# Seven-product stage of h kept in program order, with two attention visits a period and the second pair's x sums on VectorE in place

## The chip, the cores and the metric

The kernel runs on one core of a Trainium2 chip. TensorE (PE) multiplies, VectorE (DVE) and ScalarE (ACT) read its PSUM banks, GpSimd (POOL) works from SBUF alone, and SyncE (SP) issues the transfers. Each engine takes its instructions strictly in order, so an instruction that waits holds up all that stand behind it on that engine. The metric is the time of one execution on the device in microseconds; lower is better.

## The reference, cut to what matters

```python
state = gamma * state + einsum('bhd,bhe->bhde', k[t], v[t])   # retention, 4 batches, 8 heads, 768 tokens
y[t]  = scale * einsum('bhd,bhde->bhe', q[t], state)
x = y.transpose(0, 2, 1, 3).reshape(3072, 512)
h = x @ w_in                  # 512 -> 2048
g = h - tanh(h)
x = g @ w_out                 # 2048 -> 512
h = x @ w_in2                 # 512 -> 1024; then softmax-weighted h, layer norm, @ w_out2 -> 512
```

All is fp32. A product of two fp32 tiles is taken as three matmuls: each tile is split into a high part (a cast to fp32r on ACT) and the low rest (a subtraction on DVE), and the products high by high, high by low and low by high are added in PSUM.

## The kernel before

Attention works in 24 units: six chunks c of 128 tokens by four batches b. A unit is visited twice by PE. The first visit, "sc", forms the scores and the new state, which DVE turns into `pr`, `sb` and `sa` (L327 to L338). The second, "out", forms the outputs; ACT copies them from the two banks into x (`xf`, L299), and DVE adds the second part from the same banks (L307). Both visits use the same two PSUM banks (pool `ps_a`), so the next sc visit can start only when the copies and the additions of the visit before are done.

The tokens lie in six blocks of 512 (`SB`). The product h = x @ w_in is done for two blocks at a time (a pair) against two tiles of w_in, with seven products P1 to P7 for each two-by-two block of tiles instead of eight (L758, six matmuls of 128x128 by 128x512 each). The seven need sums and differences of the tiles of w_in (`wsum`, L544 to L547, class `Factors`) and of x (`x_sums`, L605, L610 on DVE and L601 on POOL), and each of these is split into high and low (`wch`/`wcl`, `xh`/`xl`, by `parts`, L165 and L166; `put_x` does it for x).

The stage of h that the change touches has 16 periods n. Periods 0 to 7 work on the first pair (blocks 2 and 3) against eight groups j of w_in, and 8 to 15 on the second pair (blocks 4 and 5) against the same groups, stored to DRAM (`wcd`, `store_w`) and loaded again (`load_wl`). A period issues P2(n), P5(n), P4(n-1), P6(n), P3(n-1), P1(n+1) and P7(n), in banks of a pool of six (`ps_h`). P1, P5 and P6 are read from their bank by ACT into `part` (`keep`, L768), because the bank goes on being added to. `summed` (DVE, L784) adds bank and part to `hs`; `finish` takes the tanh (ACT, L774) and the difference (L776, on POOL after P2, P3 and P7, on DVE after P4), and the result `g` goes to DRAM (`gd`). The buffers for `part`, `hs`, `th` are a ring of 15 (`t2`), those for weights and x a ring of 40 (`t4`); SP keeps at most eight transfers under way.

In the same periods the last 16 attention visits (units 16 to 23, whose x are blocks 4 and 5) stand between the products, three a period in periods 0 to 5, and `Factors(n+1)` prepares the weights of the next period. In the last period, the first `gp` (splits of g loaded back) and `w` (splits of w_out) for the following stage, x = g @ w_out (`py`, L382), are made.

The order on PE and SP is that of the program. What ACT, DVE and POOL do in this stage is put in order by the framework's scheduler when the program is built; an instruction that goes through `pin(..., True)` keeps its place in program order among the others that do, and `fix` does so where `late[0]` is set. Before, `late[0]` is set only near the end of the kernel.

Of the kernel before, what the change touches and what calls it, by code (L numbers as in the profile page):

```python
# [36 lines left out]
P = 128  # L37
# [52 lines left out]
def body(ctx: ExitStack, tc, z, w_in, w_out, w_in2, w_out2, g_ln, cst, tab, out):  # L90
# [144 lines left out]
    def prepare(k, own, wide=False, fixed=True):  # L235
# [12 lines left out]
        ), wide and fixed)  # L248
        src = zv[k][:, 1, :, :].rearrange("q p (h d) -> q (p h) d", h=2)
        c0 = C_VS + c * H  # L250
        for h in range(own):
            pin(nc.scalar.activation(
                v[:, h, :], src[:, h, :], AF.Copy, scale=con[:, c0 + h : c0 + h + 1]
            ), wide and fixed)
        if own < H:
            pin(nc.gpsimd.tensor_tensor(
                v[:, own:, :], src[:, own:, :],
                con[:, c0 + own : c0 + H].unsqueeze(2).to_broadcast([P, H - own, D]), ALU.mult,
            ), wide and fixed)
        vs[k] = v  # L260

    def unit(ko, ks, hold=False, pool=ps_r, tag="r", opool=ps_r, engs=None, amid=None):
# [4 lines left out]
        if ko is not None:  # L267
# [29 lines left out]
            if c:  # L297
                for h in range(2):
                    pin(nc.scalar.copy(xf[:, h, :, :], fr[h]), amid)  # L299
            else:  # L300
                for h in range(2):
                    pin(nc.scalar.copy(xf[:, h, :, rows(1)], fr[h][:, :, rows(1)]), amid)
                pin(nc.scalar.copy(xa[:, :, rows(0)], ya[0]), amid)
            if amid:
                amid()
            for ab in steps:
                pin(nc.vector.tensor_tensor(  # L307
                    xa[:, :, rows(ab)], xa[:, :, rows(ab)], ya[ab], ALU.add
                ), amid)
            if not hold:  # L310
                split_x(c, b, xf, engs or (nc.gpsimd, nc.gpsimd), amid)
        if ks is not None:
# [13 lines left out]
            for h in range(2):  # L326
                pin(nc.vector.tensor_tensor(  # L327
                    pr[:, h, :, :], sc[h], mask.unsqueeze(1).to_broadcast([P, NP, D]), ALU.mult
                ), amid)
            pt[ks] = pr  # L330
            sb[ks] = stp.tile([P, NP, D], F32, tag="sb", name="sb", bufs=3)
            if c == 0:
                nc.scalar.copy(sb[ks], gn[0])
            else:
                nc.vector.tensor_tensor(sb[ks], sa[ks], gn[0], ALU.add)
            if c < NC - 1:
                sa[ks + B] = stp.tile([P, NP, D], F32, tag="sa", name="sa")
                nc.vector.tensor_tensor(sa[ks + B], sb[ks], gn[1], ALU.add)  # L338
# [193 lines left out]
    class Factors:  # L532
# [6 lines left out]
        def sums(self):  # L539
# [4 lines left out]
            nc.vector.tensor_tensor(t[:, 0, :], a21, a22, ALU.add)  # L544
            nc.vector.tensor_tensor(t[:, 1, :], t[:, 0, :], a11, ALU.subtract)
            nc.vector.tensor_tensor(t[:, 2, :], a11, a21, ALU.subtract)
            nc.vector.tensor_tensor(t[:, 3, :], a12, t[:, 1, :], ALU.subtract)  # L547

        def split(self, i):
            g, half = divmod(i, 2)  # L550
            if half == 0:
                self.parts[g][:] = [t4([P, 4, 256], F32R, "wc" + n) for n in "hl"]
# [6 lines left out]
            h, o = (u[:, 2 * half : 2 * half + n, :].rearrange(flat) for u in self.parts[g])  # L559
            parts(h, o, src, nc.vector)  # L560
# [6 lines left out]
    def combine_w(j):  # L567
        w = Factors(j)
        w.sums()
        for i in range(4):  # L570
            w.split(i)
# [21 lines left out]
    def x_sums(p, step):  # L593
# [3 lines left out]
        def apart(out, a, b):  # L597
            for i in range(2):
                for k in range(0, SB, SB // 2):
                    at = slice(k, k + SB // 2)  # L600
                    nc.gpsimd.tensor_tensor(out[:, i, at], a[:, i, at], b[:, i, at], ALU.subtract)  # L601

        if step == 0:
            t1 = t4([P, 2, SB], F32, "xt")
            nc.vector.tensor_tensor(t1, b12, b11, ALU.subtract)  # L605
            apart(b12, b22, b12)
            sums[p] = {P1: b11, P2: b21, P3: b22, P5: t1, P7: b12}
        else:
            t2_, t4_ = (t4([P, 2, SB], F32, "xt") for _ in range(2))
            nc.vector.tensor_tensor(t2_, b22, sums[p][P5], ALU.subtract)  # L610
# [125 lines left out]
    visits = []  # L736
    for k in range(4 * B, NU):
        visits += [("sc", k), ("out", k)]
    per = [[] for _ in range(NJ1)]
    for i, v in enumerate(visits):  # L740
        per[i // 3].append(v)

    def visit(v):
        kind, k = v
# [21 lines left out]
    def keep(ph):  # L766
        t = t2([P, SB], F32, "part")
        nc.scalar.copy(t, ph)  # L768
        return t

    def finish(s, f, h, eng):

        th = t2([P, SB], F32, "th")
        nc.scalar.activation(th, h, AF.Tanh)  # L774
        g = th if eng is nc.vector else h
        eng.tensor_tensor(g, h, th, ALU.subtract)  # L776
# [5 lines left out]
    def summed(ph, part):  # L782
        h = t2([P, SB], F32, "hs")
        nc.vector.tensor_tensor(h, ph, part, ALU.add)  # L784
# [35 lines left out]
    def split_wo(f):  # L820
        wo[f] = stage3(wof[f], None, nc.vector, False)

    def begin(n):
# [3 lines left out]

    x_at = {
        (NJ1 - 1, P2): P1, (NJ1 - 1, P5): P2, (NJ1 - 1, P6): P5,
        (NJ1, P2): P6, (NJ1, P5): P7, (NJ1, P6): P4, (NJ1, P7): P3,  # L830
    }

    def after(n, m):
        if (n, m) in ((NJ1 - 2, P5), (NJ1 - 1, P2)):
            x_sums(2, n - (NJ1 - 2))
        if (n, m) in x_at:
            put_x(2, x_at[n, m], nc.vector)

    begin(0)
    for n in range(len(q) + 1):  # L840
        now, was = n < len(q), n > 0
        p, j = q[n] if now else (NSB, 0)
        todo = list(per[j]) if p == 1 else []
# [3 lines left out]

        def piece(i):
            if new:
                new.split(i) if i >= 0 else new.sums()  # L850
# [9 lines left out]
        if n == len(q) - 1:  # L860
            for i in range(2):
                split_p(i)
                split_wo(i)
        if now:
            b3 = bank()
            product(wl[n], p, P2, b3)
            finish(2 * p, j, summed(b3, p1.pop(n)), nc.gpsimd)
            piece(-1)
            after(n, P2)
            b2[n] = bank()  # L870
# [3 lines left out]
            piece(0)  # L874
            after(n, P5)
            if todo:
                visit(todo.pop(0))
        if n == len(q):
# [3 lines left out]
            split_p(2)  # L882
            split_wo(2)
            products_y(0, gp.pop(0), wo[0], py)
        if was:
# [3 lines left out]
            after(n - 1, P4)  # L889
        if now:  # L890
            product(wl[n], p, P6, b1[n], False)
            u2[n] = keep(b1[n])
            piece(1)
            after(n, P6)
            if todo:
                visit(todo.pop(0))
        if was:
            product(wl.pop(n - 1), pp, P3, b2[n - 1], False)
            finish(2 * pp + 1, jj, summed(b2.pop(n - 1), u2.pop(n - 1)), nc.gpsimd)
            after(n - 1, P3)  # L900
        if now:
            if n + 1 < len(q):
                piece(2)
                begin(n + 1)
                after(n + 1, P1)
# [4 lines left out]
            if todo:  # L910
                visit(todo.pop(0))
# [157 lines left out]

    bank_of = []  # L1070
# [207 lines left out]
```

## Time and profile before

| what | value |
|---|---|
| times of three runs | 849.32, 852.65, 852.97 us; median 852.65 |
| the profiled execution | 848.72 us, its span 846.9 us, granted clock 0.998 |
| PE busy / chain of waits on PE | 96% / 83% of the span |
| stage of h by seven, from its first product to the end of its last | 237.68 to 423.61 us |
| its matmuls (128x512) | 672, and 16 attention visits of 64 small matmuls |

The span is the time from the first to the last instruction that the profiler recorded. PE's records overlap because matmuls are pipelined, so its share of busy time does not show how long it waited; the rows on waits and the chain do. "Idle before" names what ended an idle stretch, taken from semaphore events, and it is not always the true cause.

### The profile page before, as it was taken

The page shows a single profiled execution, that of the slowest core. Times are in us where ns is not written, and L with a number is a line of the kernel's source. Part 1 is how long each engine was busy: PE and PEld are TensorE (multiplying, and loading weights), DVE is VectorE, ACT ScalarE, POOL GpSimd, SP SyncE. Part 2 cuts the span into 40 slices and gives each one's busy share as a digit, 9 for nine tenths or more (in the row PEclk, how much of TensorE's full clock was granted, in tenths as well). Part 3 has the DMA queues.
Part 4 walks back from the last instruction along what each step waited for, and adds up shares of the span by engine and source line. Part 5 has one row for each costly group of instructions (what it writes and reads, how often), then busy time and mean ns, then how long its engine had stood idle before and what let it go on. Part 6 is the DMA issues. An engine that isn't in the chain of part 4 may idle for free.

```text
span 846.9 us, 16439 instructions
## 1 busy us (share of the span) xinstructions
PE 816.8 (96%) x6296; PEld 672.5 (79%) x6296; DVE 552.9 (65%) x1000; ACT 470.4 (56%) x880; POOL 308.3 (36%) x304
## 2 busy tenths in 40 slices
PE   5699999999999989999999999999999999999998
PEld 5678888788877777888788888888788888888876
DVE  3788875999866858322562897483666656566571
ACT  4556644556456546444562445353667677667762
POOL 4511200090635339344400260061655555545310
PEclk9999999999999999999999999999999999999999
DMA  9658754452899825963592919380887777776694
GB/s 362 248 217 312 264 200 124 129 184 99 300 364 339 318 77 172 394 267 130 205 345 104 321 44 318 100 285 14 177 169 153 150 150 149 150 150 124 125 188 86
DMA packets 168606, 169.43 MB, mean 200 GB/s; under 512 B 105680, under 2 KB 118224, under 8 KB 168528
## 3 DMA queue, kind: packets, MB, share of 16 engines
q1 hardware_dynamic: 160176, 153.51, 60.4%
q10 hardware_dynamic: 8352, 14.87, 5.1%
q8 instruction: 49, 0.80, 0.4%
q14 instruction: 29, 0.24, 0.1%
HBM read 107.02 MB, written 61.34 MB: 199 GB/s over the span
## 4 chain that ended last, share of the span: by engine, by line
PE 83%; DVE 6%; DMA 4%; issue 3%; ACT 3%; POOL 1%; SPq 0%; ACTq 0%; DVEq 0%; POOLq 0%
PE py L382 29%; PE po L1015 15%; PE ph L758 14%; PE ph L930 12%; PE ph L357 8%; PE out L233 2%; PE sc L233 2%; DMA z<-z 1%; DMA raw<-w_in 1%; DMA wcd<-wch 1%; DMA wf<-wod 1%; DVE ex L964 1%; POOL hs L776 1%; DVE wf L139 1%; DVE wf L142 0%
## 5 line engine op out<-in xcount | busy, mean ns | idle before, releaser
L382 PE MATMUL py<-gp,w 128*128 128x512 f32 x768 | 175.6, 389 | 1.5 <-DVE gp L166 1.1
L382 PEld LDWEIGHTS py<-gp,w 128*128 128x128 f32 x768 | 144.1, 188 | 32.1 <-DVE gp L166 1.5
L1015 PE MATMUL po<-w,uh 128*128 128x512 f32 x384 | 106.7, 389 | 0.0
L776 POOL TENSOR_TENSOR hs<-hs,th 128x512 f32<-128x512 f32 x48 | 66.6, 1392 | 94.4 <-ACT th L774 86.4
L1015 PEld LDWEIGHTS po<-w,uh 128*128 128x128 f32 x384 | 72.0, 188 | 15.3 <-ACT uh L999 0.3
L357 PE MATMUL ph<-xh,w 128*128 128x512 f32 x256 | 82.1, 395 | 0.9 <-DVE w L155 0.9
L382 PE MATMUL py<-gh,w 128*128 128x512 f32 x256 | 79.3, 390 | 0.3 <-ACT gh L370 0.3
L154 ACT CAST w<-wf 128x512 fp32r<-128x512 f32 x70 | 43.0, 620 | 57.7 <-DVE wf L145 47.4
L166 DVE TENSOR_TENSOR gp<-g,gp 128x512 fp32r<-128x512 f32 x64 | 48.4, 766 | 25.4 <-ACT gp L165 25.3
L774 ACT ACTIVATE th<-hs 128x512 f32<-128x512 f32 x48 | 30.3, 631 | 61.4 <-DVE hs L784 56.4
L1015 PE MATMUL po<-w,ul 128*128 128x512 f32 x192 | 63.0, 389 | 0.0
L155 DVE TENSOR_TENSOR w<-wf,w 128x512 fp32r<-128x512 f32 x70 | 51.2, 736 | 14.7 <-ACT w L154 13.9
L930 PE MATMUL ph<-w,yhs 128*128 128x512 f32 x192 | 59.2, 390 | 0.7 <-ACT part L937 0.7
L758 PE MATMUL ph<-xh,wch 128*128 128x512 f32 x140 | 56.5, 403 | 1.6 <-DVE hs L784 1.6
L357 PEld LDWEIGHTS ph<-xh,w 128*128 128x128 f32 x256 | 48.0, 188 | 11.9 <-DVE w L155 1.3
L382 PEld LDWEIGHTS py<-gh,w 128*128 128x128 f32 x256 | 48.0, 188 | 10.6 <-ACT gh L370 0.7
L784 DVE TENSOR_TENSOR hs<-ph,part 128x512 f32<-128x512 f32 x48 | 32.9, 686 | 35.6 <-PE ph L758 23.0
L165 ACT CAST gp<-g 128x512 fp32r<-128x512 f32 x64 | 38.7, 617 | 29.5 <-DMA g<-gd 18.9
L758 PE MATMUL ph<-xh,wcl 128*128 128x512 f32 x140 | 54.7, 390 | 0.0
L758 PE MATMUL ph<-xl,wch 128*128 128x512 f32 x140 | 54.6, 390 | 0.0
L758 PE MATMUL ph<-xh,wc 128*128 128x512 f32 x168 | 53.1, 391 | 0.7 <-ACT part L768 0.6
L1003 DVE TENSOR_TENSOR ul<-hn,uh 128x1024 fp32r<-128x1024 f32 x24 | 32.0, 1333 | 31.0 <-ACT uh L999 31.0
(125 smaller groups left out, 1776.5 us busy)
## 6 DMA issues: line engine op xcount, KB each, us to landing
z<-z SPq DMA_DIRECT2D x48, 512.0 KB, 6.8
g<-gd SPq DMA_DIRECT2D x64, 256.0 KB, 5.3
raw<-w_in SPq DMA_DIRECT2D x24, 512.0 KB, 6.5
raw<-w_out SPq DMA_DIRECT2D x24, 512.0 KB, 4.6
gd<-hs SPq DMA_DIRECT2D x48, 256.0 KB, 3.4
ud<-ut SPq DMA_DIRECT2D x24, 512.0 KB, 3.4
hn<-ud SPq DMA_DIRECT2D x24, 512.0 KB, 6.9
y1d<-ysb SPq DMA_DIRECT2D x24, 256.0 KB, 3.8
```

The source lines that it names most:

```text
L154: pin(nc.scalar.copy(hi, wf), fixed)
L155: pin(eng.tensor_tensor(lo, wf, hi.bitcast(F32), ALU.subtract), fixed)
L165: fix(nc.scalar.copy(h, src))
L166: fix(eng.tensor_tensor(o, src, h.bitcast(F32), ALU.subtract))
L233: pin(nc.tensor.matmul(o, a, b, start=True, stop=True, skip_group_check=True), held[0])
L357: nc.tensor.matmul(ph, a[:, k, :], x, start=n == 0, stop=n == 3 * NK - 1), s < 2
L382: nc.tensor.matmul(py[e], a[:, cols], x, start=f == 0 and n == 0, stop=f == NF1 - 1 and n == 2)
L758: nc.tensor.matmul(ph, a, x, start=first and n == 0, stop=n == 5, skip_group_check=True)
L776: eng.tensor_tensor(g, h, th, ALU.subtract)
L784: nc.vector.tensor_tensor(h, ph, part, ALU.add)
L930: nc.tensor.matmul(ph, x[:, r, :], w, start=first and n == 0, stop=n == 5, skip_group_check=True)
L1015: nc.tensor.matmul(po, a[:, f, :], dec2.w[f][lo], start=n == 0, stop=n == len(todo) - 1)
```

## The change

Seven edits, all in the stage of h by seven:

1. `late[0]` is set for the whole stage, and its instructions go through `fix`: ACT, DVE and POOL follow the program's order there.
2. The attention visits go by a table: three each in periods 0 and 1, then two a period in periods 2 to 6: sc after P5, out after P7.
3. `Factors.split` is taken apart into a cast (ACT) and a low part (DVE), each placed by itself, and the weight sums come after P4 instead of after P2.
4. The x sums of the second pair are formed by DVE alone, in place in `xf`, in four steps (`late_x`), instead of two on DVE and eight quarter-size ones on POOL.
5. The splits of the second pair's x are spread: P1 and P2 go to periods 3 and 4, the five others stay in periods 7 and 8.
6. In the last period the splits of g and w_out are spread between the products.
7. After the stage `late[0]` is cleared.

```diff
-    for i, v in enumerate(visits):
-        per[i // 3].append(v)
+    visits = {
+        (0, P2): ("sc", 0), (0, P6): ("out", 0), (0, P7): ("sc", 1),
+        (1, P5): ("out", 1), (1, P6): ("sc", 2), (1, P7): ("out", 2),
+    }
+    for k in range(3, 8):
+        visits[k - 1, P5] = ("sc", k)
+        visits[k - 1, P7] = ("out", k)
...
+        def cast(self, i):
+            if i % 2 == 0:
+                self.parts[i // 2][:] = [t4([P, 4, 256], F32R, "wc" + n) for n in "hl"]
+            (h, _), src = self.pieces(i)
+            fix(nc.scalar.copy(h, src))
+        def low(self, i):
+            (h, o), src = self.pieces(i)
+            fix(nc.vector.tensor_tensor(o, src, h.bitcast(F32), ALU.subtract))
...
+    def late_x(step):
+        x0, x1 = xf_of[4], xf_of[5]
+        b11, b21, b12, b22 = (x[:, h, :, :] for x in (x0, x1) for h in range(2))
+        if step < 2:
+            at = slice(step * SB // 2, (step + 1) * SB // 2)
+            for o, x, y in ((b11, b12, b11), (b12, b22, b12)):
+                fix(nc.vector.tensor_tensor(o[:, :, at], x[:, :, at], y[:, :, at], ALU.subtract))
+        elif step == 2:
+            t = t4([P, 2, SB], F32, "xt")
+            fix(nc.vector.tensor_tensor(t, b22, b11, ALU.subtract))
+            sums[2][P6] = t
+        else:
+            fix(nc.vector.tensor_tensor(b21, b21, sums[2][P6], ALU.subtract))
     x_at = {
-        (NJ1 - 1, P2): P1, (NJ1 - 1, P5): P2, (NJ1 - 1, P6): P5,
-        (NJ1, P2): P6, (NJ1, P5): P7, (NJ1, P6): P4, (NJ1, P7): P3,
+        (3, P3): P1, (4, P3): P2, (NJ1 - 1, P5): P5, (NJ1 - 1, P6): P6,
+        (NJ1, P2): P7, (NJ1, P6): P4, (NJ1, P7): P3,
     }
+    sum_at = {(5, P3): 0, (NJ1 - 1, P2): 1, (NJ1 - 1, P4): 2, (NJ1, P5): 3}
...
+    late[0] = True
     begin(0)
...
-        if n == len(q) - 1:
-            for i in range(2):
-                split_p(i)
-                split_wo(i)
+        if new:
+            new.cast(0)
         if now:
             b3 = bank()
             product(wl[n], p, P2, b3)
-            finish(2 * p, j, summed(b3, p1.pop(n)), nc.gpsimd)
-            piece(-1)
+            h = summed(b3, p1.pop(n))
+            if new:
+                new.low(0)
+            finish(2 * p, j, h, nc.gpsimd)
             after(n, P2)
+            visit(n, P2)
...
+            visit(n, P5)
+            if final:
+                split_p(0)
...
+        if new:
+            new.sums()
         if now:
             product(wl[n], p, P6, b1[n], False)
             u2[n] = keep(b1[n])
-            piece(1)
+            if new:
+                new.cast(1)
+            visit(n, P6)
             after(n, P6)
+            if new:
+                new.cast(2)
+            if final:
+                split_wo(0)
...
         if was:
             product(wl.pop(n - 1), pp, P3, b2[n - 1], False)
-            finish(2 * pp + 1, jj, summed(b2.pop(n - 1), u2.pop(n - 1)), nc.gpsimd)
+            h = summed(b2.pop(n - 1), u2.pop(n - 1))
+            if new:
+                new.low(1)
+                new.low(2)
+            finish(2 * pp + 1, jj, h, nc.gpsimd)
...
             product(wl[n], p, P7, b1[n], False)
-            piece(3)
-            finish(2 * p + 1, j + NJ1, summed(b1[n], p5.pop(n)), nc.gpsimd)
+            h = summed(b1[n], p5.pop(n))
+            finish(2 * p + 1, j + NJ1, h, nc.gpsimd)
+            if new:
+                new.low(3)
+            visit(n, P7)
             after(n, P7)
...
+    late[0] = False
```

The order on the engines, at the three places that the prediction speaks of. A number behind a name tells buffers apart. In the changed kernel L796 is `summed` (L784 before), L788 the difference in `finish` (L776), L567 the low part of a weight (L166), L780 `keep` (L768) and L786 the tanh (L774). First, VectorE from P3 of the period that holds the out visit of unit 21 to the sc visit of unit 22, before:

```order
L784 TENSOR_TENSOR hs_4053<-ph_3685,part_3770 128x512
L166 TENSOR_TENSOR wcl_4451<-wsum_4345,wch_4450 128x512
L544 TENSOR_TENSOR wsum_4477<-wq_4343 128x256
L546 TENSOR_TENSOR wsum_4477<-wq_4343 128x256
L166 TENSOR_TENSOR wcl_4451<-wsum_4345,wch_4450 128x512
L545 TENSOR_TENSOR wsum_4477<-wsum_4477,wq_4343 128x256
L784 TENSOR_TENSOR hs_4080<-ph_3828,part_3928 128x512
L547 TENSOR_TENSOR wsum_4477<-wq_4343,wsum_4477 128x256
L166 TENSOR_TENSOR wcl_4505<-wq_4343,wch_4504 128x512
L166 TENSOR_TENSOR wcl_4505<-wq_4343,wch_4504 128x256
L307 TENSOR_TENSOR xf_3972<-xf_3972,out_4086 128x4x64
L307 TENSOR_TENSOR xf_3972<-xf_3972,out_4087 128x4x64
```

and in the changed kernel:

```order
L796 TENSOR_TENSOR hs_4155<-ph_3871,part_3954 128x512
L567 TENSOR_TENSOR wcl_4044<-wq_3851,wch_4043 128x256
L567 TENSOR_TENSOR wcl_4147<-wsum_4042,wch_4146 128x512
L166 TENSOR_TENSOR xl_4164<-xf_3368,xh_4163 128x1024
L796 TENSOR_TENSOR hs_4183<-ph_3978,part_4067 128x512
L567 TENSOR_TENSOR wcl_4147<-wsum_4042,wch_4146 128x512
L307 TENSOR_TENSOR xf_4035<-xf_4035,out_4190 128x4x64
L307 TENSOR_TENSOR xf_4035<-xf_4035,out_4191 128x4x64
L796 TENSOR_TENSOR hs_4241<-ph_4234,part_4174 128x512
```

`hs_4053` and `hs_4155` are the sums of P3, `hs_4080` and `hs_4183` those of P7; the two additions into `xf` free the banks for the sc visit. Of the eight weight operations ahead of them three are left, and a split of x (`xl_4164`) has come among them; the next weight's sums stand behind the sc visit.

Second, VectorE from period 7 to 8, where the second pair's x is made (`xl` is the low part of a piece of x, `xt` a sum). Before:

```order
L784 TENSOR_TENSOR hs_4444<-ph_4144,part_4223 128x512
L166 TENSOR_TENSOR xl_4594<-xf_3368,xh_4593 128x1024
L784 TENSOR_TENSOR hs_4471<-ph_4281,part_4370 128x512
L166 TENSOR_TENSOR xl_4607<-xf_3368,xh_4606 128x1024
L784 TENSOR_TENSOR hs_4485<-ph_4478,part_4461 128x512
L166 TENSOR_TENSOR xl_4629<-xt_4508,xh_4628 128x1024
L776 TENSOR_TENSOR th_4520<-ph_4281,th_4520 128x512
L166 TENSOR_TENSOR xl_4687<-xt_4586,xh_4686 128x1024
L784 TENSOR_TENSOR hs_4540<-ph_4363,part_4434 128x512
L166 TENSOR_TENSOR xl_4700<-xf_3972,xh_4699 128x1024
L166 TENSOR_TENSOR xl_4722<-xt_4587,xh_4721 128x1024
```

and in the changed kernel, where L847, L850 and L853 are the sums made in place:

```order
L796 TENSOR_TENSOR hs_4584<-ph_4577,part_4523 128x512
L847 TENSOR_TENSOR xf_3368<-xf_4035,xf_3368 128x2x256
L847 TENSOR_TENSOR xf_4035<-xf_4035 128x2x256
L166 TENSOR_TENSOR xl_4602<-xf_3368,xh_4601 128x1024
L788 TENSOR_TENSOR th_4611<-ph_4349,th_4611 128x512
L850 TENSOR_TENSOR xt_4615<-xf_4035,xf_3368 128x1024
L166 TENSOR_TENSOR xl_4626<-xt_4615,xh_4625 128x1024
L796 TENSOR_TENSOR hs_4635<-ph_4428,part_4496 128x512
L796 TENSOR_TENSOR hs_4656<-ph_4516,part_4599 128x512
L796 TENSOR_TENSOR hs_4677<-ph_4670,part_4648 128x512
L166 TENSOR_TENSOR xl_4684<-xf_4035,xh_4683 128x1024
L853 TENSOR_TENSOR xf_3368<-xf_3368,xt_4615 128x1024
```

The `xl` of P1 and P2 have gone to periods 3 and 4, and three steps of the sums stand among the five that are left (L850 makes `xt_4615`, which L853 takes away from `xf_3368`).

Third, ScalarE at the start of the last period, before:

```order
L774 ACTIVATE th_5209<-ph_5065 128x512
L768 COPY part_5219<-ph_5146 128x512
L154 CAST w_5257<-wf_5175 128x512
L165 CAST gp_5260<-g_5169 128x512
L154 CAST w_5263<-wf_5177 128x512
L165 CAST gp_5338<-g_5171 128x512
L154 CAST w_5341<-wf_5179 128x512
L165 CAST gp_5395<-g_5173 128x512
L774 ACTIVATE th_5229<-hs_5227 128x512
```

and in the changed kernel:

```order
L165 CAST gp_5270<-g_5161 128x512
L786 ACTIVATE th_5279<-ph_5140 128x512
L780 COPY part_5289<-ph_5227 128x512
L154 CAST w_5291<-wf_5169 128x512
L786 ACTIVATE th_5302<-hs_5300 128x512
L165 CAST gp_5306<-g_5163 128x512
L786 ACTIVATE th_5317<-hs_5315 128x512
L154 CAST w_5321<-wf_5171 128x512
L786 ACTIVATE th_5350<-ph_5227 128x512
```

Six casts in a row have become single casts between the reads of the banks.

## Rows read from the trace of the kernel before

**Rows 1.** The page: the chain that ended last, share of the span by engine

```profile
PE 83%; DVE 6%; DMA 4%; issue 3%; ACT 3%; POOL 1%; SPq 0%; ACTq 0%; DVEq 0%; POOLq 0%
```

**Rows 2.** Chain of the stage, in order of time: start us, us, what

```profile
237.68 4.08 PE ph L758 x18
...
304.64 4.31 PE ph L758 x18
308.95 1.09 PE sc L233 x64
...
423.61 4.53 PE py L382 x20
```

**Rows 3.** Waits of PE, 230 to 430 us: us in total, times, longest

```profile
PE sc L233 <- POOL hs L776: 2.8, 1, 2.8
PE ph L758 <- DVE hs L784: 1.6, 1, 1.6
PE out L233 <- DVE sa L338: 0.9, 1, 0.9
PE ph L758 <- ACT part L768: 0.6, 1, 0.6
PE sc L233 <- issue: 0.6, 1, 0.6
```

**Rows 4.** Timeline around 299 us, engine by engine: start us, us, engine, line, operation

```profile
299.04 1.18 PE L233 MATMUL sc<-vq,z 64*64 64x64 f32 x43 [2.83 <-POOL hs L776]
...
295.36 0.93 ACT L165 CAST wch<-wq 128x512 fp32r<-128x512 f32 x2 [1.81 <-DVE wcl L166]
...
296.84 0.63 ACT L299 COPY xf<-out 128x256 f32<-128x256 f32 x2
...
296.52 2.08 DVE L166 TENSOR_TENSOR wcl<-wq,wch 128x512 fp32r<-128x512 f32 x2
298.53 0.74 DVE L307 TENSOR_TENSOR xf<-xf,out 128x256 f32<-128x256 f32 x2
...
297.01 1.32 POOL L776 TENSOR_TENSOR hs<-hs,th 128x512 f32<-128x512 f32 x1 [2.56 <-ACT th L774]
```

**Rows 5.** Timeline of DVE and POOL, 321 to 336 us

```profile
321.54 1.21 DVE L166 TENSOR_TENSOR xl<-xf,xh 128x1024 fp32r<-128x1024 f32 x1
...
332.00 2.31 DVE L166 TENSOR_TENSOR xl<-xt,xh 128x1024 fp32r<-128x1024 f32 x1
...
321.58 5.94 POOL L601 TENSOR_TENSOR xt<-xf,xt 128x256 f32<-128x256 f32 x4
327.47 7.97 POOL L776 TENSOR_TENSOR hs<-hs,th 128x512 f32<-128x512 f32 x4
```

**Rows 6.** Timeline of ACT in the last period

```profile
407.70 0.62 ACT L154 CAST w<-wf 128x512 fp32r<-128x512 f32 x1 [0.94 <-DMA wf<-wod]
...
410.32 0.61 ACT L165 CAST gp<-g 128x512 fp32r<-128x512 f32 x1
```

**Rows 7.** Groups by line and shape, 237.5 to 423.5 us: count, busy us, mean ns, idle before

```profile
L776 POOL TENSOR_TENSOR hs<-hs,th 128x512 f32<-128x512 f32 x47 | 65.3, 1394 | 90.2 <-ACT th L774 82.3 <-DMA gd<-th 4.1 <-DMA g<-gd 3.3
L784 DVE TENSOR_TENSOR hs<-ph,part 128x512 f32<-128x512 f32 x47 | 32.2, 685 | 35.6 <-PE ph L758 23.0 <-POOL hs L776 6.2 <-ACT th L774 3.1
L327 DVE TENSOR_TENSOR pr<-sc,con 128x256 f32<-128x256 f32 x16 | 6.7, 419 | 2.9 <-PE sc L233 2.9
L307 DVE TENSOR_TENSOR xf<-xf,out 128x256 f32<-128x256 f32 x16 | 6.0, 414 | 9.4 <-ACT xf L299 9.4
```

**Rows 8.** Stretches of the stage: busy us of PE, PEld, DVE, ACT, POOL; clock, DMA share, GB/s

```profile
252.00:267.00 15.00, 14.98 (x240) 11.85 (x239) 9.92 (x17) 7.84 (x22) 8.20 (x8) 1.00 1.00 371
267.00:282.00 15.00, 14.37 (x237) 11.30 (x236) 12.93 (x27) 8.31 (x19) 5.77 (x6) 1.00 0.88 298
...
327.00:342.00 15.00, 13.38 (x60) 10.74 (x59) 11.16 (x10) 8.92 (x14) 12.76 (x8) 1.00 0.79 263
```

**Rows 9.** Timeline of POOL before the stage

```profile
215.56 9.45 POOL L245 TENSOR_TENSOR vq<-z,tab 128x512 f32<-128x512 f32 x1 [23.44 <-DVE gl L373]
```

More of the change, by code (lines that the diff above doesn't have):

```diff
@@ L247, in prepare @@
             zq[k][:, 0, :, :].rearrange("q p t -> q (p t)"), tb[c], ALU.mult,
-        ), wide and fixed)
+        ), wide and fixed or late[0])
         src = zv[k][:, 1, :, :].rearrange("q p (h d) -> q (p h) d", h=2)
@@ L253, in prepare @@
                 v[:, h, :], src[:, h, :], AF.Copy, scale=con[:, c0 + h : c0 + h + 1]
-            ), wide and fixed)
+            ), wide and fixed or late[0])
         if own < H:
@@ L258, in prepare @@
                 con[:, c0 + own : c0 + H].unsqueeze(2).to_broadcast([P, H - own, D]), ALU.mult,
-            ), wide and fixed)
+            ), wide and fixed or late[0])
         vs[k] = v
@@ L543, in sums, with pieces @@
             )
[L544 to L549, printed above, removed]
+            fix(nc.vector.tensor_tensor(t[:, 0, :], a21, a22, ALU.add))
+            fix(nc.vector.tensor_tensor(t[:, 1, :], t[:, 0, :], a11, ALU.subtract))
+            fix(nc.vector.tensor_tensor(t[:, 2, :], a11, a21, ALU.subtract))
+            fix(nc.vector.tensor_tensor(t[:, 3, :], a12, t[:, 1, :], ALU.subtract))
+        def pieces(self, i):
             g, half = divmod(i, 2)
-            if half == 0:
-                self.parts[g][:] = [t4([P, 4, 256], F32R, "wc" + n) for n in "hl"]
             flat = "p a c -> p (a c)"
@@ L570, in combine_w @@
         for i in range(4):
-            w.split(i)
+            w.cast(i)
+            w.low(i)
     def store_w():
@@ L735, in body, with visit @@
     ps_a = G.enter_context(tc.tile_pool(name="ps_a", bufs=2, space=PSUM, reuse_waits="tile"))
[L736 to L739, printed above, removed]
-    for i, v in enumerate(visits):
-        per[i // 3].append(v)
-    def visit(v):
-        kind, k = v
+    visits = {
[5 more added lines that the diff above has]
+        visits[k - 1, P7] = ("out", k)
+    def visit(n, m):
+        if (n, m) not in visits:
+            return
+        kind, k = visits[n, m]
+        k += 4 * B
         if kind == "sc":
@@ L767, in keep @@
         t = t2([P, SB], F32, "part")
-        nc.scalar.copy(t, ph)
+        fix(nc.scalar.copy(t, ph))
         return t
@@ L846, in body @@
         new = Factors(n + 1) if 1 <= n < NJ1 - 1 else None
-        def piece(i):
-            if new:
-                new.split(i) if i >= 0 else new.sums()
+        final = n == len(q) - 1
         if n == NJ1 - 1:
```

69 lines of the change are left out of this document (35 added, 34 removed).

## The prediction, made before the changed kernel was run

> **What bounds the kernel now.** I read the page's chain of waits first. It gives PE 83% of the span [rows 1], so PE sets the time nearly everywhere and another engine counts only where PE stands still for it. The change touches one stage, so the chain of that stage comes next. From the first product at 237.68 to the end of the last at 423.61, where the next stage takes over, it lasts 185.93 us [rows 2]. An undisturbed run of 18 matmuls takes 4.08 us, 0.2267 each [rows 2]. Three products and an attention visit, without a wait, take 4.31 + 1.09 = 5.40, of which 4.08 is matmuls, so a visit costs 1.32 [rows 2]. The stage holds 672 matmuls (152.3), 12 of the next stage that stand inside it (2.7) and 16 visits (21.1): 176.1 us. The other 9.8 us are stalls, and the change can win no more, because it leaves PE the same instructions. The list of PE's waits names five, 6.5 us in all [rows 3]. The other 3.3 lie in the slower restart after each of them and in gaps too small for that list. The granted clock is 1.00 in every stretch I looked at [rows 8], so nothing is to be had from it.
>
> **The two waits of sc, 2.8 and 0.6.** The list puts the longer one down to POOL's hs. I take that for a coincidence in time: what the sc visit needs is its two banks, and these come free when DVE has added them into xf. At 299 us ACT's copies began only at 296.84, because a weight cast stood ahead of them until 295.36, waiting 1.81 us for DVE. DVE then ran two weight splits, 296.52 for 2.08 us, beside POOL's hs at 297.01, and began the additions at 298.53; sc began at 299.04, between the first addition and the second [rows 4]. So the weights' work ahead of the copies and the additions made the stall. In the new order it stands behind: on ACT the copies follow the tanh of P7, on DVE one split stands between the hs of P7 and the additions. Counted from the start of P7, out ends at 1.36 + 1.32 = 2.68, the copies (0.63) end near 3.5, the additions (0.74) near 4.3 [rows 4], and sc starts at 2.68 + 2 x 1.36 = 5.4. That leaves about 1.1 us, and I cost the two waits at nothing.
>
> **The same slack in periods 3, 4 and 5.** DVE's load there is what I trust least. In the busiest stretch of before it was busy 12.93 us of 15 [rows 8]. A period with three visits lasts 42 x 0.2267 + 3 x 1.32 = 13.5, so that is 11.6 us a period, and it holds the time in which DVE was itself held up. One visit less takes off at least two operations of 0.414 [rows 7]: 10.8, in a new period of 42 x 0.2267 + 2 x 1.32 = 12.2. In periods 3 and 4 an xl is added, in period 5 a step of the sums, which has as many elements. One such operation took 1.21 alone and 2.31 beside POOL [rows 5]. The sum is 12.0 to 13.1 of 12.2, so each of the three loses between nothing and 0.9 us. I take 0.4 each, 1.2, somewhat below the middle, because POOL has three hs of 1.39 and the two vq operations of the next unit, which I count as no longer than hs: at most 7.0 of 12.2 [rows 7].
>
> **The wait of out for sa, 0.9.** It is in period 0, where out waits for the state that sc has just made. Before, sc stood after P5 and out after P6, one product of 1.36 between them; now sc stands after P2, so that two products lie between, 1.36 more than the wait. I expect it to go. Period 1 gains the first pieces of its weights, which before were made earlier, beside three visits: the load that the 11.6 of 13.5 us describes, so nothing is added.
>
> **The wait on hs at the second pair, 1.6.** Before, seven xl and two sums for DVE and eight operations of a quarter of their size for POOL fell into little more than two periods. POOL was busy 12.76 of 15 there [rows 8], four hs took it 7.97, and xl took 2.31 in place of 1.21 [rows 5]. POOL loses its x work. Two of the seven xl go to periods 3 and 4. Periods 7 and 8 keep five, and have the second step of the sums (two halves that make one), t and one subtraction: 8 operations of 1.21, 4 a period, 4.8 us. With three hs of 0.685 [rows 7] and the difference after P4, which I count like them, 2.7, DVE has 7.6 us in periods of 42 x 0.2267 = 9.5. If every x operation took 2.31 it would be 12.0, and the two periods would lose 5.0. Followed through in order, P4(7), P4(8) and P3(8) are the products that have least to spare: the hs of P7(7), that of P7(8) and the last xl come between 1 us early and 1 us late for them. POOL is now busy 4.2 of 9.5 instead of 12.76 of 15, so I take 1.0, nearer to the lower end of 0 to 5.
>
> **The rule of the Trainium skill that speaks against this part** is in "SBUF — State Buffer", section "Who interferes with whom": a VectorE instruction with two SBUF inputs and a GpSimd instruction that reads SBUF shut each other out, and the one that comes second waits until the other is through. The rows bear the waiting out in both directions: the xl of 2.31, and POOL's 9.45 us for one operation while DVE ran such operations one after another [rows 5, 9]. By the rule alone the new in-place sums, all with two SBUF inputs, can still be held for one hs each, at most 1.39; what it would do in full is the last rival.
>
> **The last period, 0.6.** ACT had six casts in a row from 407.70 to 410.93, ahead of the tanh and the copies that free the banks [rows 6]; PE's wait for part follows in that period [rows 3]. Spread singly, each delays a copy by 0.62, and a bank is wanted at the earliest a product of 1.36 after the one that filled it. Cost nothing; if the loads of g and w_out come late the casts hold ACT instead, which has both ends of 0 to 0.9, since that is what such a wait on the neighbouring transfer was [rows 6].
>
> **Sum.** 9.8 of stalls, of which I leave 0.3 in place as small gaps; against it 1.2 and 1.0: 7.3 us won. The profiled execution took 848.72, 1.8 outside its span; the change touches nothing there. It becomes 841.4. The median of the runs shown lies 3.9 higher, at 852.65, and the runs' own lowest is 849.32. At that level it is 845.3, which I give.
>
> **Rivals.**
> *Only part comes off.* The bare periods fit DVE by 0.2 us, and a late addition holds sc in each of the five periods with two visits. Periods 3 to 5 lose 0.9 each and the second pair 3.5: 6.2 new against 9.5, 3.3 won, 849.3. For it: the 2.31 and the 12.93. Against it: POOL has less to do.
> *The transfers bind.* A period issues two loads of z and one of weights (512 KB each), stores of weights of 1792 KB and of g of 1024 KB: 4352 KB, 4.46 MB in 12.2 us, 365 GB/s. The trace moved 371 and 298 GB/s in two neighbouring stretches [rows 8]. At the mean, 334, a period would last 13.3, and six such periods 6.6 more; the ring of buffers gives back part, and nothing much is won: 852. Against it: at 298 the transfer engines were busy 0.88, so it was the demand that fell.
> *All comes off.* 9.8 won, nothing new: 842.9 at the median's level, 838.9 at the profiled one's.
> *Slower: POOL and DVE lock each other out.* The place is DVE in periods 2 to 8: in the written order its operations on two SBUF inputs (weights, x sums, xl) follow each hs of its own, just when POOL starts on the one before. If each of three hs (4.2) is added to DVE's 10.8, a period is 15.0 for 12.2: 2.8 more in each of five, and in the second pair's two 7.6 + 4.2 = 11.8 for 9.5, 2.3 each: 18.6 in all, 9.1 more than is won, 861.8. It decides once DVE is held more than 1.4 us a period, and turns to a loss from about 2.8. Against it: 11.6 already contains what POOL held up. This is the Trainium skill's rule above at its full price.
>
> **Chances.** The forecast 0.54, all off 0.06, a part 0.16, the transfers 0.13, slower 0.08, something else 0.03. What a measurement of this kernel can tell from no change is about 0.5%, 4.3 us. Faster by more than that: the first two and a third of the third, with a little off for runs that lie high, 0.65. Slower by more: 0.09. The rest, 0.26. The forecast's own range is 839.5 to 848.5. To hold the time 8 times in 10 the range begins at 839.0, where all comes off at the profiled level, and ends at 851.5, which takes in the part and half of the transfers' case.
>
> **What would show it.** The stage lasts 178 to 179 us from first product to the start of the next stage. PE's list has no wait of sc above 1 us; what remains of sc's waits is in periods 3 to 5. DVE's xl take 1.2 to 1.5 us. If the sc waits stay and the records show the xf additions late, the first rival holds; if weight stores land later than 9 us after issue and ACT's casts wait for wq, the second. I am wrong altogether if the stage is shorter but the time is not, or if waits appear after the stage.

## The result and the profile after

| | median | runs | lowest to highest |
|---|---|---|---|
| before, runs beside it | 850.19 us | 6 | 847.46 to 852.97 |
| changed | 842.16 us | 6 | 840.15 to 844.91 |

The ratio is 0.9903, with a 95% interval of 0.9881 to 0.9925: 8.0 us less. The profiled execution of the changed kernel took 840.54 us with a span of 838.7, which is 8.2 less than the two numbers of before.

The chain on the changed kernel's page begins at 805 us of 838.7, so it covers only the last 4% of the span and does not reach the stage, so the stage is read from PE's timeline. These rows (start us, us, engine, line, operation, idle before) are its first matmul, the one wait in it that the list of waits names, and the first py matmul behind it; the last line is that list:

```profile
237.29 0.39 PE L770 MATMUL ph<-xh,wch 128*128 128x512 f32 x1
...
412.06 0.50 PE L770 MATMUL ph<-xh,wc 128*128 128x512 f32 x1 [0.33 <-DVE hs L796]
...
414.93 1.30 PE L382 MATMUL py<-gp,w 128*128 128x512 f32 x5
...
PE ph L770 <- DVE hs L796: 0.3, 1, 0.3
```

The stage lasts 414.93 - 237.29 = 177.64 us. Measured the same way it was 185.93 before, so 8.29 us went here, all that the profiled execution lost. Five waits of 6.5 us in sum [rows 3] have become one of 0.33. What lies before and behind the stage is the same within a few tenths (237.5 and 423.5 us before, 237.3 and 423.8 after).

The place of the long sc wait [rows 4], again behind period 3, on DVE, ACT and PE (the visit there is now that of unit 21; unit 22's comes a period later):

```profile
285.79 1.48 DVE L166 TENSOR_TENSOR xl<-xf,xh 128x1024 fp32r<-128x1024 f32 x1 [0.77 <-ACT xh L165]
287.19 0.68 DVE L796 TENSOR_TENSOR hs<-ph,part 128x512 f32<-128x512 f32 x1
287.79 0.68 DVE L567 TENSOR_TENSOR wcl<-wsum,wch 128x512 fp32r<-128x512 f32 x1
289.16 0.75 DVE L307 TENSOR_TENSOR xf<-xf,out 128x256 f32<-128x256 f32 x2 [0.69 <-ACT xf L299]
...
288.50 0.63 ACT L299 COPY xf<-out 128x256 f32<-128x256 f32 x2
...
290.02 1.18 PE L233 MATMUL sc<-vq,z 64*64 64x64 f32 x64
```

ACT's copies now follow the tanh at once, and DVE's additions (289.16 to 289.91) are through 0.1 us before sc starts. That is the whole margin behind period 3; it is 1.2 behind period 2, where no xl is made, and 0.1 again behind period 4. In period 5 the first step of the x sums (two operations) stands at this place, and sc loses 0.3:

```profile
309.53 2.51 DVE L847 TENSOR_TENSOR xf<-xf 128x512 f32<-128x512 f32 x2
...
313.87 0.75 DVE L307 TENSOR_TENSOR xf<-xf,out 128x256 f32<-128x256 f32 x2 [0.63 <-ACT xf L299]
...
326.37 1.41 DVE L847 TENSOR_TENSOR xf<-xf 128x512 f32<-128x512 f32 x2
...
309.48 1.29 POOL L788 TENSOR_TENSOR hs<-hs,th 128x512 f32<-128x512 f32 x1 [2.81 <-ACT th L786]
...
314.45 1.46 PE L233 MATMUL sc<-vq,z 64*64 64x64 f32 x64
```

The same pair of operations, for the other half of x, takes 1.41 us where POOL is not at work when it starts; the first takes 2.51 right behind POOL's start at 309.48: held for 1.1, the length of POOL's operation less a little. The Trainium skill's "SBUF — State Buffer", "Who interferes with whom", says that a VectorE instruction with two SBUF inputs contends with a GpSimd instruction that reads SBUF, and that the second to issue waits until the first is through. The trace agrees, and the price here is a little less than one hs.

Stretches of the stage, to be held against [rows 8] (busy us of PE, PEld, DVE, ACT, POOL; clock, DMA share, GB/s):

```profile
281.00:296.00 15.00, 15.00 (x184) 12.13 (x183) 11.82 (x24) 10.19 (x22) 5.92 (x6) 1.00 0.99 356
296.00:311.00 15.00, 15.00 (x218) 11.93 (x221) 12.17 (x22) 10.07 (x21) 7.00 (x6) 1.00 0.69 257
327.00:342.00 15.00, 15.00 (x68) 12.43 (x67) 10.68 (x12) 9.07 (x15) 5.47 (x4) 1.00 0.61 218
```

PE is busy all through these stretches. POOL, 12.76 of 15 at the second pair before, is at 5.47. The transfers ran at 356 GB/s with a share of 0.99, close to the 365 that the prediction worked out as wanted, and PE waited for none of them.

### The profile page after: what moved, and what is told of

Same layout as the page of the kernel before. It is cut to its first block, busy times and chain, and to the rows that moved or that the text cites. A ratio compares the mean times of both kernels' runs of the same rounds, so it can differ in the third digit from the quotient of the medians.

```text
span 838.7 us, 16423 instructions
## 1 busy us (share of the span) xinstructions
PE 813.5 (97%) x6296; PEld 670.2 (80%) x6296; DVE 547.4 (65%) x1004; ACT 471.9 (56%) x880; POOL 294.5 (35%) x296
## 5 line engine op out<-in xcount | busy, mean ns | idle before, releaser
L788 POOL TENSOR_TENSOR hs<-hs,th 128x512 f32<-128x512 f32 x48 | 62.6, 1306 | 118.1 <-ACT th L786 110.8
L166 DVE TENSOR_TENSOR gp<-g,gp 128x512 fp32r<-128x512 f32 x64 | 49.3, 780 | 25.9 <-ACT gp L165 25.8
L786 ACT ACTIVATE th<-hs 128x512 f32<-128x512 f32 x48 | 30.4, 632 | 54.0 <-DVE hs L796 52.4
L796 DVE TENSOR_TENSOR hs<-ph,part 128x512 f32<-128x512 f32 x48 | 32.8, 687 | 30.0 <-PE ph L770 17.4
```

The lines of the kernel that those rows point to most:

```text
L166: fix(eng.tensor_tensor(o, src, h.bitcast(F32), ALU.subtract))
L788: fix(eng.tensor_tensor(g, h, th, ALU.subtract))
L796: fix(nc.vector.tensor_tensor(h, ph, part, ALU.add))
```

## The experiments

All are read by the length of the stage in the profiled execution, measured as above. The whole time varies by some 4 to 7 us between executions of one kernel, and up to 2.7 of that lies ahead of the stage (last section). Each length comes from one execution: where a slower clock is part of it, the text says how much, and differences under 1 us rest on the waits found in the records more than on the length.

| kernel | stage us | median of its runs, us |
|---|---|---|
| before | 185.93 | 850.2 to 850.9 beside the others |
| changed | 177.64 | 842.16 |
| changed, scheduler's order | 182.80 | 847.76 |
| before, program order only | 193.26 | 858.36 |
| changed, three visits a period | 178.13 | 843.31 |
| changed, x sums as before | 179.31 | 843.81 |
| changed, x sums in place on POOL | 181.16 | 845.40 |
| changed, last period as before | 178.51 | 844.11 |
| changed, sums again ahead of the additions | 186.65 | 850.46 |
| changed, sums again behind sc | 181.75 | 845.93 |
| order and weights' places only | 182.10 | 846.42 |
| changed, weights at their old places | 187.92 | 851.46 |
| before, one POOL operation on DVE | 188.09 | 849.87 |
| changed, two more moves | 177.77 | 841.53 |

**Is it the order? The scheduler's order in the changed kernel.**

```diff
-    late[0] = True
     begin(0)
```

> The changed kernel, but the scheduler orders ACT, DVE and POOL in the stage again; the table of visits, the x sums in place and the spread splits stay. Measure: the stage from its first product to the first py product after its last (185.93 us before, 177.64 in the changed kernel). Theory A (the place of the weight operations ahead of the copies and additions that free the two banks made the long sc wait): the scheduler pulls weight sums and splits ahead of the additions again, two sums' worth of waits of 1 to 3 us come back at sc, stage 180 to 184. Rival B (two visits a period and less POOL work are what matters, the order is secondary): stage 177 to 178.5.

182.80: theory A. The order is worth 5.2 us of the 8.3. The waits of sc are back, at three places, and with them the wait for part in the last period. At the longest of them DVE has three of the four weight sums ahead of the additions again:

```profile
PE sc L233 <- issue: 2.6, 3, 1.1
PE ph L770 <- ACT part L780: 0.6, 1, 0.6
PE out L233 <- DVE sa L338: 0.6, 1, 0.6
...
307.96 0.41 DVE L544 TENSOR_TENSOR wsum<-wq 128x256 f32<-128x256 f32 x1
308.29 0.41 DVE L546 TENSOR_TENSOR wsum<-wq 128x256 f32<-128x256 f32 x1
308.62 0.41 DVE L545 TENSOR_TENSOR wsum<-wsum,wq 128x256 f32<-128x256 f32 x1
309.33 0.75 DVE L307 TENSOR_TENSOR xf<-xf,out 128x256 f32<-128x256 f32 x2 [0.29 <-ACT xf L299]
...
309.85 1.52 PE L233 MATMUL sc<-vq,z 64*64 64x64 f32 x64 [1.06 <-issue]
```

**Is it any order? The kernel before, kept in its own program order.** The edit sets `late[0]` for the stage and puts the stage's instructions through `fix`.

> The kernel before with nothing changed but that the stage is kept in program order: three visits a period, the weights' casts and splits where the code of before has them, x sums and splits as before. Theory A: an order that was not made for the visits does not free the banks in time either; the code has the four weight sums right behind the hs of P2, where in a period of three visits sc or out follow at once; stage 181 to 190, so little or nothing won. Rival C (program order by itself suffices): stage 177 to 180.

193.26, 7.3 longer than before and beyond what theory A expected. Some 3 us of it are a slower clock (eleven matmuls started 0.43 us apart and one 0.59, in place of 0.227, and the sc visit ahead of three of them was stretched by 0.6; last section). The rest are waits that the profile puts down to every engine: vq on POOL, pr and sb on DVE, part on ACT, x. So keeping program order, with the program as it was, is worse than the scheduler's order.

**What made the order good? The places of the weights' work.** Two runs, one from either side. The first takes of the change the order and the weights' new places only:

```diff
+    visits = {}
+    for i in range(16):
+        visits[i // 3, (P5, P6, P7)[i % 3]] = (("sc", "out")[i % 2], i // 2)
...
+        if (n, m) in ((NJ1 - 2, P5), (NJ1 - 1, P2)):
+            x_sums(2, n - (NJ1 - 2))                   # with the old x_at
...
+        if final:
+            for i in range(2):
+                split_p(i)
+                split_wo(i)
```

> Of the change only the program order and the new places of the weights' casts, splits and sums; three visits a period, x sums and the last period's splits as before. What the earlier runs cost one by one against the changed kernel's 177.64: visits 0.5, x 1.7, end 0.9. Theory E (the places of the weights make the order worth keeping, the other edits add): 177.6 + 3.1 = 180.7, so 180 to 181.5. Rival (the edits need one another, as the order alone at 193.3 may suggest): 185 or more.

182.10, 0.6 above what theory E expected and 2.9 under the rival's 185: against the run with the order only, which differs in the weights' places and in one pair of splits at the very end of the stage, 11.2 us less (some 3 of them clock). No wait of sc is left. Together with the other three edits, 4.5 more come off; taken off the changed kernel one by one these cost 0.5, 1.7 and 0.9. The other 1.4 comes from their working together or from the old x sums, which stand after P5 of period 6 here and after P7 in the run that tests them by themselves; no run parts the two. The second run leaves everything as changed but puts the weights' work back:

```diff
-            new.cast(0) ... new.low(0) ... new.sums() ... new.cast(1) ... new.low(3)
+            piece(-1)   # sums behind the hs of P2
+            piece(0)    # each cast with its low part, after P5, P6, P3 and P7
```

> The changed kernel with the weights' work at its old places in the program (sums right behind the hs of P2, each cast with its split, before the hs or the copies of the same product), all else as changed: two visits, in-place x sums, order kept. Theory E: ACT's and DVE's in-order waits for one another come back, as in the run with the order only (193.26): stage 184 to 192. Rival F (two visits and x sums made the room, so the weights may stand anywhere): 177.6 to 180.

187.92: theory E, 10.3 us more (about 1.5 of it clock: three matmuls 0.43 apart, one 0.59, and the sc visit ahead of them stretched by 0.5). The rows of DVE, ACT and PE at the sc of period 4 show how the wait builds up:

```profile
288.26 0.68 DVE L796 TENSOR_TENSOR hs<-ph,part 128x512 f32<-128x512 f32 x1
290.63 1.48 DVE L166 TENSOR_TENSOR xl<-xf,xh 128x1024 fp32r<-128x1024 f32 x1 [1.69 <-ACT xh L165]
292.03 1.28 DVE L567 TENSOR_TENSOR wcl<-wsum,wch 128x512 fp32r<-128x512 f32 x2
293.24 0.68 DVE L796 TENSOR_TENSOR hs<-ph,part 128x512 f32<-128x512 f32 x1
295.14 0.75 DVE L307 TENSOR_TENSOR xf<-xf,out 128x256 f32<-128x256 f32 x2 [1.23 <-ACT xf L299]
...
294.48 0.63 ACT L299 COPY xf<-out 128x256 f32<-128x256 f32 x2
...
295.67 2.07 PE L233 MATMUL sc<-vq,z 64*64 64x64 f32 x64 [1.70 <-issue]
```

DVE stands 1.69 us for a cast of x on ACT (0.77 in the changed kernel), which had itself waited for the hs of P3. Two weight splits (292.03), the second of which the change puts behind the hs of P7, then hold that hs until 293.24; ACT's tanh and copies can only follow, DVE waits 1.23 us for the copies, and sc starts at 295.67, 1.7 late.

**Does the place of DVE's work matter, or only its amount?** Two runs compute the four sums of periods 2 to 6 a second time, with values that nobody uses: once right ahead of the out visit's additions, once right behind the sc visit's reads.

```diff
                 new.low(3)
+                if n > 1: new.sums()          # first run
             visit(n, P7)
...
             visit(n, P5)
+            if new and n > 1: new.sums()      # second run
```

> The changed kernel with the four weight sums of each of periods 2 to 6 computed a second time (same values, unused) on DVE right ahead of the out visit's two additions. The four take 1.65 us in the changed kernel's trace; 0.69 of it lies in DVE's wait for ACT's copies there; the additions end 1.2, 1.2, 0.1, 0.1 us ahead of the next sc and 0.2 behind it in periods 2 to 6. Theory A (what stands on DVE ahead of these additions decides the sc waits): nothing in the first, about 0.9 us each in the three later ones: stage 2 to 4 us longer, 179.6 to 181.6, with waits of sc in PE's list. Rival D (only DVE's total load counts): as much as in the sister run with the same extra sums placed behind the sc visit.

> The changed kernel with the same four extra weight sums, but placed on DVE right behind the reads of the sc visit after P5, where DVE waits 1.3 us for the tanh of P4 in the changed kernel. Theory A: 0 to 0.4 us a period reaches the additions, 0 to 1.2 us in all: stage 177.6 to 178.9. Rival D (load): the same as the sister run, 179.6 to 181.6.

186.65 and 181.75: the same work costs 9.0 us at one place (7.4 without the slower clock in it) and 4.1 at the other. The place matters, as theory A says, but both sizes are outside what I expected, and the amount matters too. In the second run the waits are at the sc of periods 4, 5 and 6, where the changed kernel had 0.1 us to spare twice and nothing the third time: the extra sums delay the hs of P3 and all that follows. I had counted them as 1.65; beside POOL, ahead of the sc of period 6, they took 3.2:

```profile
308.13 0.67 DVE L544 TENSOR_TENSOR wsum<-wq 128x256 f32<-128x256 f32 x1
308.84 1.40 DVE L545 TENSOR_TENSOR wsum<-wsum,wq 128x256 f32<-128x256 f32 x1
310.16 0.83 DVE L546 TENSOR_TENSOR wsum<-wq 128x256 f32<-128x256 f32 x1
310.91 0.41 DVE L547 TENSOR_TENSOR wsum<-wq,wsum 128x256 f32<-128x256 f32 x1
...
308.48 1.47 POOL L245 TENSOR_TENSOR vq<-z,tab 128x512 f32<-128x512 f32 x1
```

In the first run three waits before sc are about 1.4 us and one is short, 4.4 in all. To these come 1.6 us of slower clock behind the last and two waits at the second pair, which began late.

**Was POOL's hs what ended the long wait before, as the profile names it?** The kernel before, with the difference after P7 of period 3 on DVE; the order of everything else is the same.

```diff
-            finish(2 * p + 1, j + NJ1, summed(b1[n], p5.pop(n)), nc.gpsimd)
+            finish(2 * p + 1, j + NJ1, summed(b1[n], p5.pop(n)), nc.vector if n == 3 else nc.gpsimd)
```

> The kernel before with a single operation moved: the difference after P7 of period 3, which POOL runs at 297.01 just ahead of the long sc wait at 299.04, goes to DVE; all other orders are the same. The profile names this POOL operation as what ended the wait. Theory A (the coincidence; copies and additions into xf end it): DVE takes the operation when the tanh is done at 296.93, 0.69, then the two weight splits without POOL beside them, 1.0, so the additions begin near 298.7 instead of 298.53 and sc starts about 3.0 to 3.4 late as before (3.2). Rival (POOL's operation itself releases sc): the wait falls below 1.5.

```profile
298.46 0.69 DVE L776 TENSOR_TENSOR th<-hs,th 128x512 f32<-128x512 f32 x1 [0.36 <-ACT th L774]
299.07 1.02 DVE L166 TENSOR_TENSOR wcl<-wq,wch 128x512 fp32r<-128x512 f32 x2
300.01 0.74 DVE L307 TENSOR_TENSOR xf<-xf,out 128x256 f32<-128x256 f32 x2
...
300.52 2.35 PE L233 MATMUL sc<-vq,z 64*64 64x64 f32 x64 [2.81 <-issue]
```

The POOL operation is gone from that place and the wait is as long: 2.81 us against 2.83 [rows 3], now named "issue". The stage began 1.34 later in this execution; the additions at 300.01 are 298.67 on the clock of before, and 298.7 was expected. The copies and additions release sc, not POOL. Every trace says the same: in before and the runs of this section sc starts more than 0.2 us late 20 times, and each time its first matmul comes 0.10 us behind the end of the first of the two additions, whatever the list of waits names (POOL's hs, POOL's vq, or "issue"). (That the stage is 2.2 longer than before comes from a slower clock, last section.)

**The other edits, one by one.** Three visits a period again:

```diff
+    for i in range(16):
+        visits[i // 3, (P5, P6, P7)[i % 3]] = (("sc", "out")[i % 2], i // 2)
```

> The changed kernel with the visits of before: three a period in periods 0 to 5, after P5, P6 and P7. Theory A: the distance from an out to the next sc stays two products or more, but DVE has 11.6 us of work or blocked time in 13.5 and the adds of xl and sums come on top, so some waits of about 1 us at sc or out return: stage 179 to 183. Rival C (order alone): 177 to 178.5. If the table mattered most: 184 or more.

178.13, rival C's range and not theory A's: the table of visits is worth 0.5 us, and no wait of sc comes back. PE loses 0.7 more at the second pair (0.5 of it a wait for an xl) and 0.2 at the out of period 0, and wins the 0.4 that the changed kernel lost at sc. The x sums as before, and in place on POOL:

```diff
+        if (n, m) in ((NJ1 - 2, P7), (NJ1 - 1, P2)):
+            x_sums(2, n - (NJ1 - 2))                   # first run, with the old x_at
...
-                fix(nc.vector.tensor_tensor(o[:, :, at], x[:, :, at], y[:, :, at], ALU.subtract))
+                fix(nc.gpsimd.tensor_tensor(o[:, :, at], x[:, :, at], y[:, :, at], ALU.subtract))   # second
```

> The changed kernel with the second pair's x made as before: sums on DVE (two) and POOL (eight quarter operations), splits of all seven in periods 7 and 8. Theory: the wait at the second pair comes back (1.6 and its restart, 1.9 before), while the 0.4 us lost in periods 3 to 6 goes: stage 1 to 2.5 us longer, 178.6 to 180.1. Rival (the x sums were not the point, the order was): 177 to 178.

> The changed kernel with the in-place sums of the second pair's x on POOL instead of DVE, same places and order. POOL took 1.39 for 128x512 where DVE takes 0.68 to 1.25, so the pair of half sums is 2.6 to 2.8 and t and the subtraction as much each; the splits behind them wait. Theory: 1 to 4 us longer, with waits of PE on hs in periods 7 and 8; stage 178.6 to 181.6. Rival (the lock between DVE and POOL is what costs, so with DVE lighter it evens out): 177 to 178.

179.31 and 181.16, both as the theory has it. In the first the wait at the second pair is back at its old 1.6, this time named xl; in the second POOL needs 3.39 us for what DVE does in 1.21, and the hs behind it are late. The last period as before (four splits at its start):

> The changed kernel with all four splits of g and w_out at the start of the last period, as before. The prediction's step has 0.6 us of wait and its restart here, 0.9 in all before; in the changed kernel a wait of 0.33 (0.6 with the restart) is left in the last period. Expected 0.2 to 0.9 longer than the changed kernel's stage, 177.9 to 178.5. Rival: the six casts in a row were harmless and the wait came from elsewhere: 177.0 to 177.7.

```profile
PE ph L770 <- ACT part L780: 1.2, 1, 1.2
```

178.51, 0.9 longer, at the upper end of what was expected.

**A version with two more moves**: the split of g that DVE ran ahead of the hs of P7 in the last period goes behind it, and the first step of the x sums goes to period 6.

```diff
-    sum_at = {(5, P3): 0, ...
+    sum_at = {(6, P3): 0, ...
             h = summed(b1[n], p5.pop(n))
             finish(2 * p + 1, j + NJ1, h, nc.gpsimd)
+            if final:
+                split_p(1)
```

> The changed kernel with two more moves: the second split of g in the last period comes behind the hs of P7, and the first step of the x sums goes from period 5 to period 6, behind which no sc follows. Left in the changed kernel's stage are a restart of 0.5 in the last period, 0.3 at the sc of period 6 and 0.4 in period 9. Expected: the first two go, stage 176.7 to 177.1; the time 0.5 to 1.0 us below the changed kernel's, less than the runs can tell apart.

177.77, not shorter. Both waits that the moves aimed at are gone, 0.9 us, but the second pair now loses 1.5 us where the changed kernel lost 0.4, in a wait for its last xl and smaller gaps. These rows are that wait in the list and DVE of this run; the last is the start of the same chain in the changed kernel:

```profile
PE ph L770 <- DVE xl L166: 0.5, 1, 0.5
...
324.11 2.51 DVE L847 TENSOR_TENSOR xf<-xf 128x512 f32<-128x512 f32 x2
326.54 0.68 DVE L796 TENSOR_TENSOR hs<-ph,part 128x512 f32<-128x512 f32 x1
...
333.90 1.21 DVE L850 TENSOR_TENSOR xt<-xf 128x1024 f32<-128x1024 f32 x1
...
330.53 1.21 DVE L850 TENSOR_TENSOR xt<-xf 128x1024 f32<-128x1024 f32 x1
```

From the start of xt (L850) to the end of the last xl the chain takes 18.2 us in both. It begins 93.2 us into the stage in the changed kernel and 94.0 here, because the step moved to period 6 (2.51 us beside POOL) now stands ahead of that period's last hs and additions; and PE, without the 0.3 lost at sc, comes earlier. What was won at sc is asked for again here. The median, 841.53 (839.97 to 844.52), can't be told from the changed kernel's.

## Why the prediction was right

It gave 845.3, 839.0 to 851.5, with 7.3 us won; measured are 842.16 and 8.0, and 8.29 in the stage. Of the 3.1 us between the two times 2.5 are the level: the median of before was 852.65 in the runs at hand and 850.19 with three more. The mechanism held; that the sum of its terms came within 1 us is in part luck, since two of them were 0.8 and 0.6 too dear and one 0.6 too cheap. Of its signs, the stage is 177.64 where 178 to 179 was named, no wait of sc is left above 0.3, and five of the seven xl took 1.2 to 1.5 us; the other two took 2.07 and 1.73 beside POOL.

- *The stalls of 9.8 us.* Right: 1.5 are left over the 176.1 that PE needs.
- *Sc waits for copies and additions, not for POOL's hs.* Shown, by the operation taken off POOL, by the sums put ahead of the additions and by the 0.10 us between the first addition and sc in all late visits.
- *DVE in periods 3 to 5, 0.4 each.* Too dear: 0.02, 0.06 and 0.30 were lost. The term was mis-sized at its root. I scaled DVE's busiest 15 us of before to a period and got 12.0 to 13.1 us with xl; DVE is busy 12.17 of 15 now, 9.9 a period of 12.2. In the stretch that I scaled, the scheduler had run weights ahead, and operations were stretched beside POOL. And the load was the wrong measure: DVE is idle for 2 us in such a period and yet has 0.1 to spare at the additions, because what counts is the chain from the hs of P3 to them.
- *The second pair, 1.0.* 0.4 was lost, POOL being less busy as argued; the run with the old sums gives the edit 1.7.
- *The last period, nothing.* 0.6 is left. Each cast does delay ACT by 0.62 only, but the low part behind it takes DVE 1.37 beside POOL, ahead of the hs that PE waits for. The prediction priced ACT there and left DVE out:

```profile
410.03 1.37 DVE L166 TENSOR_TENSOR gp<-g,gp 128x512 fp32r<-128x512 f32 x1 [1.27 <-ACT gp L165]
411.33 0.68 DVE L796 TENSOR_TENSOR hs<-ph,part 128x512 f32<-128x512 f32 x1
...
409.56 1.29 POOL L788 TENSOR_TENSOR hs<-hs,th 128x512 f32<-128x512 f32 x1 [4.32 <-ACT th L786]
```

- *The two visits a period.* The prediction divided its sum by waits and not by edits, and took the table as what makes room. It is worth 0.5; the weights' places are worth 10 to 11 (8 to 9 without the slower clock in those runs), and without them the order loses 7, of which some 3 are clock.
- *The rivals.* PE waited for no transfer at 356 GB/s, but with the transfer engines at a share of 0.99 there was little to spare. POOL and DVE did hold each other, up to 1.1 us at a time. It happened ahead of each of the three places where PE still lost time, the sc of period 6 (0.3), the second pair (0.4) and the last period (0.6); the full price of the last rival would have needed it at every hs.

## What to carry to other kernels

When the bounding engine waits for a buffer, look in the records for the instruction that really frees it and count what stands ahead of that instruction on its own engine; the name beside the wait can be a neighbour in time. Keeping program order paid here only once the program was written as the order, with as little as possible, and nothing that can wait, ahead of what frees a bank; the same switch over an order not made for it lost 7 us, some 3 of them to a slower clock behind the new waits. An engine's share of busy time doesn't say how much it can take on; the chain to the place where it is waited for does.

## What the runs showed of the hardware

After a wait, PE's granted clock fell to half, its 1.2 GHz level, in some executions. In the run with the sums ahead of the additions PE had waited about 1.4 us before sc three times within 30 us; behind the third, matmuls started 0.43 us apart instead of 0.227, for some 3 us. Stretches of that run (the clock is the third number from the end):

```profile
320.00:324.00 4.00, 2.49 (x68) 1.87 (x67) 3.88 (x9) 1.22 (x3) 0.98 (x2) 0.96 0.18 69
325.00:326.00 1.00, 1.00 (x4) 0.81 (x3) 0.00 (x0) 0.00 (x0) 0.00 (x0) 0.50 0.37 139
327.00:328.00 1.00, 1.00 (x6) 0.78 (x4) 0.97 (x3) 0.03 (x1) 0.00 (x0) 0.95 0.00 0
```

The same happened in the run with one POOL operation on DVE, from the sc at 300.52 to about 306.4, which cost it some 2.5 us behind a wait of 2.81, and not in the profiled execution of before, whose wait at that place was as long. So in some executions a wait cost about twice its length. In the changed kernel's profiled execution no wait in the stage is above 0.33 us and the clock is 1.00 all through it; whether it falls there in other executions isn't shown.

A part of the spread between executions goes with the same clock at the start. In the 14 profiled executions the stage began between 237.3 and 240.0 us: between 237.3 and 238.5 in the six with a clock of 1.00 at 40 to 60 us, and between 237.8 and 240.0 in the eight with 0.91. What lies behind the stage took 423.4 to 424.5. First the changed kernel, then the one with two more moves, which began at 239.9:

```profile
40.00:60.00 20.00, 19.25 (x182) 15.53 (x181) 16.07 (x31) 10.02 (x22) 3.83 (x4) 1.00 0.67 253
```

```profile
40.00:60.00 20.00, 18.43 (x173) 15.04 (x173) 13.22 (x27) 9.08 (x20) 3.90 (x4) 0.91 0.66 247
```

An edit worth less than 2 us is therefore better read from the length of its stage, and the waits and the clock in it, than from the whole time.
